# The tails of three weight loads are split by rows into pieces that use 3 to 15 DMA engines

## The chip, the cores and the metric

The kernel runs on one core of a Trainium2 chip, in one launch. The metric is the device time of that core in microseconds; lower is better. All data is 32-bit floating point. The time of before is the median of two runs.

## The reference

One decoding step of a block with two branches, for a batch of two sequences with one new token each and a width of 448. The first branch is attention with 16 query heads of size 256 over 8 cached key and value heads of 4,096 positions; the second is a bilinear gated unit with 1,792 hidden columns.

```python
xn = layernorm(x)
q = (xn @ wq), 16 heads of 256
p = softmax(q @ k_cache^T / 16)        # each key head serves two query heads
s = (p @ v_cache) @ wo
g = silu(((xn @ w_gate) * (xn @ w_up)) @ w_down)
out = x + s * g
```

Nearly all of the bytes are the two caches: 2 x 8 x 4,096 x 256 numbers each, 67 MB a cache. The weights are 24 MB.

## The kernel before

The work is 16 pairs of a key head and a sequence. For pair i the kernel needs `k{i}` (128 rows of 8,192 numbers) and `v{i}` (the same). They come in an order that lets one load serve two pairs: a load of 8 MB brings `v{i}` and `k{i+1}` as 128 rows of 64 KB. There are 14 of these (`vk` in the profile), into two buffers of the pool `ring`; the first key head (`first`) and the last pieces (`last0`, `last1`) are loaded by themselves.

The weights share one buffer, `slot`, one after the other: `wq0` (the queries of the first four key heads), `wg wu` (gate and up, 128 rows of 12,544 numbers, named `wgu`), `wd` (6,272 numbers a row), `wq1` and `wo` (10,752 numbers a row, three quarters of the output projection; the last quarter comes with `last1`). A weight lies in its rows as blocks of columns, and the matmuls go through the blocks in order.

`wq1` is a special case. A part of it, 256 KB, is taken out of the load of 128 rows and comes as `wqx` into 16 rows, from a source that is laid out as four times four rows with a gap, so that it isn't one run of rows.

All loads but that of `x` are issued by SyncE, in the order of the list `todo`, by the function `issue`. SyncE stops at an issue until the buffer is free: until the loads that wrote it have landed and the matmuls that read it are done. As `ring` has two buffers, one load is as a rule in flight when the next is issued behind it.

For each pair the loop does, in this order on TensorE: the values of pair i (`values`, line 274), the scores of pair i+1 (`scores`, line 243), then the softmax with VectorE and ScalarE, then whatever weight stage belongs to this i: `ffn_in` after pair 0 (line 171 with tile `s`), `ffn_out` after pair 2, `query(1)` after pair 4, `project` after pair 8. `project` for the blocks 16 to 23 of `wo` runs after the loop. The end of the kernel is the last value load in three pieces, the last quarter of the output projection (line 307), two VectorE operations and the store.

A load of `issue` is cut by columns only, at the places in `cuts`; each piece takes all 128 rows:

```python
for lo, hi in zip(cuts, cuts[1:]):
    nc.sync.dma_start(t[:, lo:hi], src[:, lo:hi])
```

Of the kernel before, what the change touches and what calls it, by code (L numbers as in the profile page):

```python
# [29 lines left out]
SIDE = 16  # L30
EXTRA = 8
EPS = 1e-5

# [4 lines left out]
def gated_decode_block(ctx: ExitStack, tc: tile.TileContext, x, first, vk, last0, last1, wq0, wq1, wqx, wo, wgu, wd, out):  # L40
    nc = tc.nc
# [20 lines left out]
    def issue(n=1):  # L62
        for names, src, cuts in todo[:n]:
            weight = names[0].startswith("w")
            if weight:
                t = slot.tile([128, PART], F32, name="slot", align_bytes=512)
            else:
                t = ring.tile([128, 2 * ROW], F32, name="ring", align_bytes=512)
            width = ROW if not weight else PART // len(names)
            for i, name in enumerate(names):  # L70
                loaded[name] = t[:, i * width:(i + 1) * width]
            for lo, hi in zip(cuts, cuts[1:]):
                nc.sync.dma_start(t[:, lo:hi], src[:, lo:hi])  # L73
            if names == ["wq1"]:
                at = src.shape[1]
                loaded["wqx"] = t[:, at:at + EXTRA * 512]
                nc.sync.dma_start(loaded["wqx"][:SIDE], wqx[:, :4])
        del todo[:n]
# [11 lines left out]
    plan(f"k{LAST + 1} v{LAST}", last0, [0, ROW, 2 * ROW])  # L90
    plan(f"v{LAST + 1} wo2", last1, [0, 4096, 7168, *(ROW + i * D for i in (0, 3, 5, 7, 8))])
    issue(3)


# [20 lines left out]
    nc.vector.scalar_tensor_tensor(sq, xc, 1.0, xc, op0=OP.mult, op1=OP.mult, accum_out=st[:, 2:3])  # L115
    nc.vector.tensor_scalar(st[:, 3:4], st[:, 2:3], 1.0 / D, EPS, op0=OP.mult, op1=OP.add)
    rstd = const.tile([B, 1], F32)
# [16 lines left out]
    for j in range(NK):  # L134
        at = 384 + j * SIDE
# [65 lines left out]
    def lift(ps):  # L201
        t = work.tile([128, D], F32, name="h")
        nc.scalar.copy(t, ps[:, :D])
        return t
# [108 lines left out]
    oT2 = const.tile([128, 1, 2, REP, W], F32)  # L313
    ss = scores(0)
    issue(2)
    p = over(softmax(*ss))
    for i in range(LAST):
        g, b = divmod(i, B)
        o = bank("o", 1)
        values(i, p[0], o)  # L320
        ss = scores(i + 1)

        issue(1 + (i + 1 in weights))
        nc.scalar.activation(ob[:, b * 4 + g if g < 4 else b * 3 + g - 4], o, AF.Copy, scale=p[1])  # L324
        if i == LAST - 1:
            cb = combine(ob, 6)
        p = softmax(*ss)
        if i < LAST - 1:
            p = over(p)
        if i == 7:  # L330
            cb = combine(ob, 8)
            for n in range(B):
                turn(oT0, cb[:, n * 256:(n + 1) * 256], 0, n, 4)
            ob = work.tile([128, 8, 512], F32, name="ob", bufs=1)
        if i in weights:
            if i == 0:
                ffn_in()
            if i == 2:
                ffn_out()
            if i == 4:  # L340
                query(1)
            if i == 8:
                project(oT0, 0, 0, EARLY)
# [6 lines left out]
    t = lift(wide)  # L350
# [72 lines left out]
```

## Time and profile before

| what | us |
|---|---|
| median of the runs | 376.75 (376.61 to 376.9) |
| the profiled execution | 376.31 |
| its span, first to last instruction | 374.5 |
| TensorE busy | 212.2 |
| VectorE busy | 63.2 |
| ScalarE busy | 36.2 |
| share of the span in which the 16 DMA engines are busy with SyncE's queue | 98.2% |

The profile is of one execution. Its busy times are sums over an engine's instructions; a DMA share is the mean over the sixteen DMA engines. A packet is one row of a transfer, or the small write that reports its completion. PE is TensorE's matmul, PEld its weight load, DVE VectorE, ACT ScalarE, SPq SyncE's sequencer, which issues the loads. Queue q1 holds SyncE's transfers, q10 the load of `x` that ScalarE issues, q8 and q14 the fetches of instructions.

### The profile page before, as it was taken

The page shows a single profiled execution, that of the slowest core. Times are in us where ns is not written, and L with a number is a line of the kernel's source. Part 1 is how long each engine was busy: PE and PEld are TensorE (multiplying, and loading weights), DVE is VectorE, ACT ScalarE, POOL GpSimd, SP SyncE. Part 2 cuts the span into 40 slices and gives each one's busy share as a digit, 9 for nine tenths or more (in the row PEclk, how much of TensorE's full clock was granted, in tenths as well). Part 3 has the DMA queues.
Part 4 walks back from the last instruction along what each step waited for, and adds up shares of the span by engine and source line. Part 5 has one row for each costly group of instructions (what it writes and reads, how often), then busy time and mean ns, then how long its engine had stood idle before and what let it go on. Part 6 is the DMA issues. An engine that isn't in the chain of part 4 may idle for free.

```text
span 374.5 us, 3254 instructions
## 1 busy us (share of the span) xinstructions
PE 212.2 (57%) x1464; PEld 62.4 (17%) x1464; DVE 63.2 (17%) x113; ACT 36.2 (10%) x56; POOL 1.2 (0%) x7
## 2 busy tenths in 40 slices
PE   1650648083762918699374666641718191909795
PEld 0110112021210202112021212200202020202232
DVE  4012030103030030300303030300211203020431
ACT  1001010001012020100101010100010101010120
POOL 1000000000000000000000000000000000000000
PEclk9986596657686786766857687765968776877899
DMA  8998999998999999999999999999999999999994
GB/s 343 441 469 378 444 453 448 448 443 377 428 443 448 434 400 447 436 441 450 420 448 441 443 394 423 444 448 441 448 400 443 448 427 413 450 409 437 409 417 184
DMA packets 4357, 158.79 MB, mean 424 GB/s; under 512 B 614, under 2 KB 744, under 8 KB 1256
## 3 DMA queue, kind: packets, MB, share of 16 engines
q1 hardware_dynamic: 4340, 158.59, 98.2%
q8 instruction: 11, 0.18, 0.2%
q14 instruction: 2, 0.02, 0.0%
q10 hardware_dynamic: 4, 0.00, 0.0%
HBM read 158.54 MB, written 0.06 MB: 423 GB/s over the span
## 4 chain that ended last, share of the span: by engine, by line
DMA 73%; PE 24%; SPq 1%; DVE 1%; issue 0%; ACT 0%; ACTq 0%
DMA ring<-vk 67%; PE o L274 12%; PE s L243 7%; DMA ring<-last 5%; PE t L177 2%; PE t L171 1%; SPq L73 1%; PE t L180 1%; DVE m L244 0%; ACT p L258 0%; PE acc L307 0%; DVE mx L251 0%; PE sm L266 0%; DVE h L371 0%; PE sm L249 0%
## 5 line engine op out<-in xcount | busy, mean ns | idle before, releaser
L274 PE MATMUL o<-ring,pT 128*32 128x512 f32 x480 | 83.4, 858 | 85.4 <-DMA ring<-vk 85.4
L243 PE MATMUL s<-ring,qT 128*32 128x512 f32 x512 | 61.1, 619 | 4.7 <-DMA ring<-first 3.1
L244 DVE TENSOR_REDUCE m<-s 128x1 f32<-128x1024 f32 x16 | 19.6, 1224 | 217.5 <-PE s L243 217.5
L274 PEld LDWEIGHTS o<-ring,pT 128*32 128x32 f32 x480 | 21.0, 150 | 139.7 <-issue 139.6
L324 ACT ACTIVATE ob<-o,su 128x512 f32<-128x512 f32 x14 | 9.6, 688 | 194.4 <-PE o L274 194.4
L258 ACT ACTIVATE p<-s,m 128x1024 f32<-128x1024 f32 x16 | 17.8, 1114 | 94.8 <-DVE m L255 94.8
L243 PEld LDWEIGHTS s<-ring,qT 128*32 128x32 f32 x512 | 17.7, 114 | 45.1 <-issue 43.5
L260 DVE STREAM_TRANSPOSE pT<-p 128x1024 f32<-128x1024 f32 x16 | 19.9, 1245 | 22.5 <-ACT p L258 22.5
L266 PE MATMUL sm<-su,add_head 128*128 128x1 f32 x32 | 7.3, 299 | 22.9 <-ACT p L258 22.9
L249 PE MATMUL sm<-ident,m 128*1 128x128 f32 x16 | 4.3, 270 | 18.9 <-DVE m L244 18.8
L171 PE MATMUL t<-slot,xnT 128*32 128x512 f32 x48 | 10.4, 1039 | 4.3 <-DMA slot<-wq 4.3
L251 DVE TENSOR_REDUCE mx<-sm 1x128 f32<-1x512 f32 x16 | 10.9, 679 | 6.3 <-PE sm L249 6.3
L254 PE MATMUL sm<-one,mx 1*128 1x1 f32 x16 | 3.5, 220 | 12.4 <-DVE mx L251 12.4
L266 PEld LDWEIGHTS sm<-su,add_head 128*128 128x128 f32 x32 | 6.0, 234 | 25.3 <-ACT p L258 24.1
L171 PE MATMUL s<-slot,xnT 128*32 128x448 f32 x48 | 7.2, 748 | 2.8 <-DMA slot<-wgu 2.8
L177 PE MATMUL t<-slot,oT 16*32 16x512 f32 x16 | 7.4, 942 | 0.0
L301 PE MATMUL wide<-slot,oT 128*32 128x448 f32 x48 | 7.1, 747 | 0.0
L249 PEld LDWEIGHTS sm<-ident,m 128*1 128x1 f32 x16 | 1.3, 79 | 33.0 <-DVE m L244 32.3
L283 PE MATMUL cb<-ob,add_blocks 128*32 128x64 f32 (+2 forms) x64 | 5.7, 481 | 0.8 <-ACT ob L363 0.8
L193 DVE STREAM_TRANSPOSE qT<-t 128x256 f32<-128x256 f32 x4 | 1.6, 428 | 25.2 <-PE t L177 14.2
L225 PE MATMUL t<-slot,hT 128*32 128x448 f32 x28 | 4.9, 812 | 0.0
L254 PEld LDWEIGHTS sm<-one,mx 1*128 1x128 f32 x16 | 2.2, 136 | 15.4 <-DVE mx L251 15.4
(70 smaller groups left out, 54.0 us busy)
## 6 DMA issues: line engine op xcount, KB each, us to landing
ring<-last SPq DMA_DIRECT2D x2, 4096.0 KB, 25.0
slot<-wgu SPq DMA_DIRECT2D x1, 6272.0 KB, 38.6
slot<-wo SPq DMA_DIRECT2D x1, 5376.0 KB
ring<-first SPq DMA_DIRECT2D x1, 4096.0 KB, 20.3
slot<-wq SPq DMA_DIRECT2D x1, 3584.0 KB, 11.1
slot<-wq SPq DMA_DIRECT2D x1, 3328.0 KB, 35.4
slot<-wd SPq DMA_DIRECT2D x1, 3136.0 KB, 36.9
ring<-last SPq DMA_DIRECT2D x1, 2048.0 KB
```

Of the source, the lines that this page charges most:

```text
L171: nc.tensor.matmul(ps[W * c:W * (c + 1), :n], xnT[:, k, :], block(NT * k + c), start=k == 0, stop=False)
L177: nc.tensor.matmul(ps[W * c:W * (c + 1), :n], xeT[:, j, :], extra[:SIDE, at:at + n], start=False, stop=j == NK - 1)
L243: nc.tensor.matmul(s[W * c:W * (c + 1), h, :], q[:, d], k[:, h, d, c, :], start=d == 0, stop=d == 1)
L244: nc.vector.tensor_reduce(m[:, 0:1], s, axis=AX.XY, op=OP.max)
L251: nc.vector.tensor_reduce(mx, sm[:1, None, :128].rearrange("p o (c j) -> p o j c", c=NT).to_broadcast([1, NT, W, NT]), axis=AX.X, op=OP.max)
L254: nc.tensor.transpose(sm[:, 128:129], mx.rearrange("p c j -> p (c j)"), one)
L258: nc.scalar.activation(p, s, AF.Exp, bias=m[:, 1:2], scale=1.0 / 16, accum_out=su[:, 0:1])
L260: nc.vector.transpose(pT.rearrange("p h n -> p (h n)"), p.rearrange("p h n -> p (h n)"))
L266: nc.tensor.matmul(sm[:, 130:131], add_head.rearrange("p a r j -> p (a r j)"), su[:, 0:1], start=True, stop=True)
L274: nc.tensor.matmul(o[W * t:W * (t + 1), :], pT[:, h, at:at + 2 * W:2], loaded[f"v{i}"][:, e * 512:(e + 1) * 512], start=e < NT, stop=e >= ...
L301: nc.tensor.matmul(wide[W * t:W * (t + 1), :D], heads(oT, i, first), loaded["wo"][:, i * D:(i + 1) * D], start=i < NT, stop=i >= LATE - NT)
L324: nc.scalar.activation(ob[:, b * 4 + g if g < 4 else b * 3 + g - 4], o, AF.Copy, scale=p[1])
```

## The change

The loads of `wgu`, `wd` and `wo` lose their last 512, 256 and 512 columns. These follow directly behind the main part as strips of 256 columns (1 KB a row), and each strip comes as two loads of some of the rows: the first 108 and the last 20 of the 128, and so on. All other loads stay as they are, `wq1` and `wqx` too. No computing instruction is added, removed or moved; SyncE's list of loads grows by ten.

```diff
+NARROW = 256
+ENDS = {"wu": [(108, 20), (117, 11)], "wd": [(119, 9)], "wo": [(125, 3), (98, 30)]}
...
-            for lo, hi in zip(cuts, cuts[1:]):
-                nc.sync.dma_start(t[:, lo:hi], src[:, lo:hi])
+            parts = [(lo, hi, (128,)) for lo, hi in zip(cuts, cuts[1:])]
+            if names[-1] in ENDS:
+                (lo, hi, _), = parts
+                mid = hi - NARROW * len(ENDS[names[-1]])
+                parts = [(lo, mid, (128,))] + [(mid + j * NARROW, mid + (j + 1) * NARROW, rows)
+                                               for j, rows in enumerate(ENDS[names[-1]])]
+            for lo, hi, rows in parts:
+                at = 0
+                for some in rows:
+                    nc.sync.dma_start(t[at:at + some, lo:hi], src[at:at + some, lo:hi])
+                    at += some
```

The order of SyncE's loads after the change, from `wgu` on:

```
wgu 128 x 12032, 108 x 256, 20 x 256, 117 x 256, 11 x 256
vk, vk
wd 128 x 6016, 119 x 256, 9 x 256
vk, vk, wq1, wqx, vk, vk, vk, vk
wo 128 x 10240, 125 x 256, 3 x 256, 98 x 256, 30 x 256
vk x 5, last (9 pieces)
```

## The prediction

> **What bounds the kernel now.** I read the page first (busy shares, DMA queues, the chain that ended last), then the windows, then the DMA issues and SyncE's own timeline.
>
> ```profile
> span 374.5 us, 3254 instructions
> PE 212.2 (57%) x1464; PEld 62.4 (17%) x1464; DVE 63.2 (17%) x113; ACT 36.2 (10%) x56; POOL 1.2 (0%) x7
> DMA packets 4357, 158.79 MB, mean 424 GB/s; under 512 B 614, under 2 KB 744, under 8 KB 1256
> q1 hardware_dynamic: 4340, 158.59, 98.2%
> q8 instruction: 11, 0.18, 0.2%
> DMA 73%; PE 24%; SPq 1%; DVE 1%; issue 0%; ACT 0%; ACTq 0%
> ```
>
> TensorE is busy 57% of the span; the sixteen DMA engines are busy 98.2% of it with one queue, SyncE's. The PE pieces of the chain are release steps: a buffer comes free, the next load is issued and then lies in the queue behind another. The windows say the same, and show the end (columns: length, busy time of PE, PEld, DVE, ACT and POOL, clock, DMA share, GB/s):
>
> ```profile
> 40.00:366.00 326.00, 193.99 (x1292) 56.43 (x1294) 54.41 (x85) 32.81 (x51) 0.00 (x0) 0.74 1.00 433
> 366.00:367.00 1.00, 1.00 (x14) 0.35 (x8) 0.00 (x0) 0.00 (x0) 0.00 (x0) 1.00 1.04 427
> 367.00:368.00 1.00, 0.79 (x7) 0.00 (x0) 0.00 (x0) 0.16 (x1) 0.00 (x0) 1.00 0.92 366
> 368.00:369.00 1.00, 0.42 (x24) 0.42 (x28) 0.00 (x0) 0.53 (x1) 0.00 (x0) 1.00 0.71 272
> 369.00:370.00 1.00, 1.00 (x42) 0.72 (x32) 0.25 (x1) 0.00 (x0) 0.00 (x0) 1.00 0.45 177
> 370.00:371.00 1.00, 0.62 (x24) 0.35 (x16) 0.00 (x0) 0.00 (x0) 0.00 (x0) 1.00 0.18 70
> ```
>
> From 40 to 366 us the share is 1.00 at 433 GB/s, or 27.1 bytes per ns and engine: no engine is ever without work, and none waits for another. So each engine's finish is the sum of what it carries, and the kernel ends with the most loaded one. The share falls over some 3.5 us at the end: the engines finish unevenly. The last landing that TensorE waits for is at 370.48:
>
> ```profile
> 171.28 5.26 PE o L274 x32
> 176.54 3.49 PE s L243 x32
> 180.03 0.02 issue
> 180.04 28.88 DMA ring<-vk
> ...
> 350.07 20.41 DMA ring<-last
> 370.48 0.04 issue
> 370.52 1.01 PE acc L307 x24
> ```
>
> Until there the average engine stands idle 0.08 + 0.29 + 0.55 + (0.48 - 0.18) = 1.2 us. That is all that a perfect levelling could bring: 0.3%.
>
> The trace also keeps each packet (one row of a transfer) with start and length. The views don't print them one by one; I strung them into sixteen chains, each packet starting where one ended, which works because a 65,536-byte row repeats every 2,415 ns. A row of S bytes takes S x 0.0368 + 4.4 ns (70 ns at 1,792 bytes, 607 at 16,384). How far each chain is behind the earliest one where the load of `k15` begins:
>
> ```
> engines                                            us behind the earliest
> 4 that carry wqx                                   2.70 2.78 3.15 3.26
> 2 that serve two of q8's code fetches              3.34 1.52 (2.94 from 350 us)
> 6 that serve one code fetch                        1.37 1.54 1.56 1.58 1.69 1.70
> 4 with neither                                     0.00 0.14 0.14 0.37
> ```
>
> `wqx` put 2.43 us on its four chains in one step, a code fetch some 1.4 us on one. The end is thus shared by the four of `wqx` and the two that are fetched on twice.
>
> **The change part by part.** The loads in question and what SyncE does around them (start, length, instruction; a merged row spans its members):
>
> ```profile
> slot<-wgu SPq DMA_DIRECT2D x1, 6272.0 KB, 38.6
> slot<-wd SPq DMA_DIRECT2D x1, 3136.0 KB, 36.9
> slot<-wo SPq DMA_DIRECT2D x1, 5376.0 KB
> slot<-wqx SPq DMA_DIRECT2D x1, 256.0 KB
> 18.54 0.33 SPq L73 DMA_DIRECT2D slot<-wgu  x1
> 26.69 23.66 SPq L73 DMA_DIRECT2D ring<-vk  x2
> 66.22 0.33 SPq L73 DMA_DIRECT2D slot<-wd  x1
> 86.62 18.52 SPq L73 DMA_DIRECT2D ring<-vk  x2
> 114.54 0.80 SPq L77 DMA_DIRECT2D slot<-wqx  x1
> 199.96 0.40 SPq L73 DMA_DIRECT2D slot<-wo  x1
> 217.73 91.36 SPq L73 DMA_DIRECT2D ring<-vk  x5
> ```
>
> *Bytes.* The three loads lose five tails of 128 rows x 1 KB; ten new loads carry the same 640 rows. No byte is added. Each of the 128-row loads runs on all engines, so a tail was 8 KB on each, 40 KB in all, or 1.51 us.
>
> *Engines.* How many a load uses shows in its completions. Of the 614 packets under 512 bytes, 128 are rows of the output and 2 belong to the load of `x`; the other 484 are completions, 30 x 16 for the thirty loads and stores of 128 rows and 4 for `wqx`, whose source is 4 x 4 rows: four engines, 64 KB each. So a load runs on the largest number up to 16 that divides its rows: 108 rows on 12 engines (9 rows each), 20 on 10 (2), 117 on 13 (9), 11 on 11 (1), 119 on 7 (17), 9 on 9 (1), 125 on 5 (25), 3 on 3 (1), 98 on 14 (7), 30 on 15 (2). If each takes the first so many in one fixed order, the 640 rows fall like this:
>
> ```
> place of the engine    1-3  4-5  6-7  8-9  10  11  12  13  14  15  16
> rows of 1 KB, after     74   73   48   31  30  28  27  18   9   2   0    (before: 40 KB each)
> ```
>
> A 1 KB row takes 37.7 + 4.4 = 42.1 ns, a completion some 7. Places 1 to 3: 74 x 42.1 + 10 x 7 = 3.19 us against 1.51, so +1.7 us; places 4 and 5: +1.6; 6 and 7: +0.6; 8 to 12: -0.15 to -0.35; 13 to 16: -0.7, -1.1, -1.4, -1.5.
>
> *Which engines.* No row says what places the four of `wqx` have, so the term is bounded from both sides: they are the first four (+1.6 to +1.7 on chains that share the end now), or the last four (-0.7 to -1.5, with the end left to others). I take the first: `wqx` is itself such a load of few engines, the nearest thing in the trace to the new ones, and the same hardware path picks for both. [...] The count of completions bears out the number of engines; which ones, no row here shows.
>
> *SyncE's queue.* `wqx`, on four engines, took 0.80 us to issue where a whole load took 0.33, so I price each new issue at 0.8: four behind `wgu` end at 22.1 us, the next load on the queue is issued from 26.69; two behind `wd` end at 68.2, the next is at 86.62; four behind `wo` end at 203.6, the next is at 217.73. Nothing queued behind them is late. Without that cover it would be 3.2 us at one place, still less than the load in flight.
>
> *New waits.* TensorE waits for the tails only ahead of the last blocks of `wu`, `wd` and `wo`: some ten waits on loads that lie in the queue directly behind the main part. PE's own reserve covers that (waited for: us in total, times, longest):
>
> ```profile
> PE o L274 <- DMA ring<-vk: 85.4, 13, 13.1
> PE s L171 <- DMA slot<-wgu: 2.8, 1, 2.8
> ```
>
> It stands 85 us before thirteen key and value loads. A tail of `wgu` that lands 1 us later still lies ahead of the last `wu` blocks, as the `wg` blocks come first.
>
> *Starving the fast engines.* The tightest issue is at 180.04: the earliest chain finishes its previous rows at 185.9, 5.9 us later. By then only `wgu` and `wd` have run, and the first seven places are 0.8 us later (39 rows of 1 KB where 24 KB were), so some 5 us are left. At the end the last pieces are issued 1.65 us later, against chains that finish the load before them from 353.3 us on, at least 2 us after the last issue. This costs nothing.
>
> *Sum.* The latest `wqx` chains end 1.65 us later, and what follows the last landing (some 4 us) stays: the profiled execution goes from 376.31 us (its span of 374.5 and 1.8 around it) to 377.96. The median of the runs is 0.44 above the profiled one, so 376.75 + 1.65 = 378.4 us, or +0.4%. That is inside the 2% that a measurement of this kernel can about tell from no change.
>
> **The rivals.**
>
> *Other engines.* The new loads start where the four idle-most chains are, and `wqx`'s four lie late in the order. Those four then gain 0.7 to 1.5 us; the chain with two fetches keeps its 3.3, less 0.15 to 0.35 if it is at places 8 to 12, plus 0.6 at 6 or 7. From -0.3 to +0.6: I put 376.5 us, with 375.5 as the floor from the 1.2 us above. For it: the two chains that start right after the two packets of `x` are not `wqx`'s. Against it: a start order blurred by up to 0.8 us.
>
> *Writes that meet.* In a whole load each engine writes rows of its own; the new pieces let an engine write rows that another engine writes at the same time in its large load. If a row's way into SBUF carries no more than one engine's 27.1 bytes per ns, every foreign row costs its 37.7 ns again: some 70 of the 74 rows, 2.6 us, so +4.3 us in all and 381.0 us; with the 40 rows that others push into the chain's own way, 1.5 more: 382.5. For it: 433 GB/s is flat whatever is in flight. Against it: nothing in this trace has two engines on one way. [...]
>
> *A stall per small load, the slower side.* Each of the ten pieces breaks the stream on its engines as the very first load does: its first rows take 1.2 to 2.2 us instead of 1.06, on average some 0.7 us lost. Ten such stalls on the first three chains: 7 + 1.65 = 8.7, so 385.4 us (+2.3%). It decides from (7.5 - 1.65) / 10 = 0.6 us per piece. Against it: the last seven loads, of 16 KB rows and less, follow each other 6 ns apart on a chain, and the window at 366 still has a share of 1.04.
>
> **How the numbers follow.** Forecast 0.60; other engines 0.22; writes that meet 0.12; stalls 0.06. The range goes from 376.3 to 381.0: it holds the forecast with its own spread (377.9 with no cost per row, 379.5 with two microseconds' worth of overlap at the ports), most of the second case, and reaches the third's price. Over 2% slower means above 384.3: the stalls and a little of the ports, 0.08. Over 2% faster means below 369.2; with 1.2 us to be had there is no way to it but an error of mine: 0.02. Within 2%: 0.90.
>
> **What would show it.** Right: the DMA share still 1.00 up to 366 us; over 100 more packets under 512 bytes (98 to 100 completions, as 12 + 10 + 13 + 11 + 7 + 9 + 5 + 3 + 14 + 15 = 99) and 640 more between 512 bytes and 2 KB; a longer slope at the end, with the share below 0.5 for about 3 us instead of 1.5; issues of about 0.8 us on SyncE. If the slope gets shorter and the span falls, the places were the other way round. If the share exceeds the bytes (1.00 at less than 433 GB/s) in the slices around 55, 100 and 240 us, rows meet on their way. If it drops below 1.00 there, pieces stall. A wait of TensorE on `slot` longer than now would say that the cover was misread.

## The result, and the profile after

The changed kernel takes 382.3 us (two runs, 380.53 and 384.08) against 376.75: a ratio of 1.015, with a 95% interval of 1.012 to 1.018. It is slower, by less than 2%, but by 5.55 us, over three times the 1.65 us of the forecast, and it lies above the range (376.3 to 381.0). The ratios here leave out any execution over 1.5% above the fastest of its kernel; in two of the experiments that drops slow stretches which belong to the kernel itself, so their single times are given too.

The profiled execution is the slower of the two, 384.08 us. From its page:

```profile
span 382.1 us, 3269 instructions
DMA packets 5096, 158.79 MB, mean 416 GB/s; under 512 B 713, under 2 KB 1483, under 8 KB 1995
q1 hardware_dynamic: 5079, 158.59, 97.8%
DMA 73%; PE 21%; another core or an unknown queue 3%; SPq 1%; issue 0%; DVE 0%
```

The bytes are the same and the engines are as busy as before, for 7.6 us longer: 416 GB/s instead of 424. The 99 new completions are there (614 to 713), so the pieces do run on as many engines as the largest divisor up to 16 says, and so are the 640 rows of 1 KB (130 to 770 packets between 512 bytes and 2 KB).

Two things are new in the windows (columns as above; the last two are the DMA share and GB/s, both counted by the packets that start in the window, so in a short one the second over the first is the rate of a working engine set). The stretches behind the three split loads:

```profile
54.00:58.00 4.00, 1.38 (x10) 0.76 (x14) 1.28 (x2) 0.00 (x0) 0.00 (x0) 0.58 1.13 393
58.00:83.00 25.00, 12.13 (x88) 2.96 (x84) 1.27 (x2) 0.53 (x1) 0.00 (x0) 0.66 1.02 396
104.00:109.00 5.00, 3.95 (x40) 0.97 (x32) 0.99 (x1) 0.69 (x1) 0.00 (x0) 1.00 1.13 434
240.00:249.00 9.00, 5.34 (x44) 1.91 (x40) 3.36 (x5) 1.76 (x3) 0.00 (x0) 0.82 1.07 387
110.00:240.00 130.00, 80.81 (x476) 22.27 (x480) 20.36 (x34) 14.16 (x22) 0.00 (x0) 0.72 1.00 431
249.00:370.00 121.00, 67.33 (x474) 20.31 (x466) 20.66 (x31) 11.24 (x19) 0.00 (x0) 0.73 1.00 430
```

The same two first windows of before:

```profile
54.00:58.00 4.00, 1.13 (x7) 0.55 (x11) 1.30 (x2) 0.06 (x1) 0.00 (x0) 0.65 1.20 520
58.00:83.00 25.00, 14.60 (x100) 3.65 (x96) 1.27 (x2) 0.53 (x1) 0.00 (x0) 0.65 0.97 420
```

The engines are not idle (share 1.02 to 1.13) but move 348, 388, 384 and 362 GB/s while they work (393 / 1.13 and so on), where before it was 433 in both. Elsewhere the rate is as ever. In the packet records rows of 64 KB take up to 3.5 us in these stretches instead of 2.42, on all sixteen chains alike. Summed over the execution, rows take 6.5 us per engine longer than the quickest of their size; before it was 1.5. That is 5.0 of the 7.6 us.

The end, and SyncE's timeline:

```profile
372.00:373.00 1.00, 0.63 (x24) 0.40 (x20) 0.25 (x1) 0.00 (x0) 0.00 (x0) 1.00 0.86 350
373.00:374.00 1.00, 1.00 (x10) 0.24 (x4) 0.00 (x0) 0.00 (x0) 0.00 (x0) 1.00 0.76 308
374.00:375.00 1.00, 1.00 (x8) 0.14 (x4) 0.00 (x0) 0.00 (x0) 0.00 (x0) 1.00 0.52 197
375.00:376.00 1.00, 0.21 (x6) 0.08 (x8) 0.00 (x0) 0.69 (x1) 0.00 (x0) 1.00 0.37 143
376.00:377.00 1.00, 1.00 (x48) 0.86 (x52) 0.25 (x1) 0.00 (x0) 0.00 (x0) 1.00 0.29 115
377.00:378.00 1.00, 0.58 (x22) 0.34 (x20) 0.00 (x0) 0.00 (x0) 0.00 (x0) 1.00 0.13 50
...
18.45 1.98 SPq L84 DMA_DIRECT2D slot<-wgu  x5
28.27 21.99 SPq L84 DMA_DIRECT2D ring<-vk  x2
203.90 1.91 SPq L84 DMA_DIRECT2D slot<-wo  x5
223.36 92.63 SPq L84 DMA_DIRECT2D ring<-vk  x5
```

The slope is longer. With the last landing on the chain at 377.82, the average engine is idle for 0.14 + 0.24 + 0.48 + 0.63 + 0.71 + (0.82 - 0.13) = 2.9 us before it, where it was 1.2: the unevenness grew by 1.7 us, as the forecast had it. SyncE needs 1.98 us for the five loads of `wgu` and is long done when the next is due.

So the term that was forecast is there, and a second one beside it. The experiments separate them.

### The profile page after: what moved, and what is told of

It is laid out like the page before. It is cut to its first block, busy times and chain, and to the rows that moved or that the text cites. A ratio compares the mean times of both kernels' runs of the same rounds, so it can differ in the third digit from the quotient of the medians.

```text
span 382.1 us, 3269 instructions
## 1 busy us (share of the span) xinstructions
PE 212.4 (56%) x1464; PEld 62.6 (16%) x1464; DVE 63.2 (17%) x113; ACT 36.2 (9%) x56; POOL 1.2 (0%) x7
## 4 chain that ended last, share of the span: by engine, by line
DMA 73%; PE 21%; another core or an unknown queue 3%; SPq 1%; issue 0%; DVE 0%
DMA ring<-vk 55%; PE o L286 11%; DMA slot<-wgu 10%; PE s L255 6%; DMA ring<-last 6%; DMA slot<-wq 3%; PE s L183 2%; PE t L183 1%; SPq L84 1%; PE s L196 0%; PE t L196 0%; PE acc L319 0%; DVE h L383 0%; DVE h L384 0%
## 5 line engine op out<-in xcount | busy, mean ns | idle before, releaser
L255 PE MATMUL s<-ring,qT 128*32 128x512 f32 x512 | 62.4, 630 | 5.1 <-DMA ring<-first 3.5
L183 PE MATMUL t<-slot,xnT 128*32 128x512 f32 x48 | 9.7, 971 | 4.1 <-DMA slot<-wq 4.1
L183 PE MATMUL s<-slot,xnT 128*32 128x448 f32 x48 | 7.1, 744 | 2.6 <-DMA slot<-wgu 2.6
```

The source lines that it names most:

```text
L183: nc.tensor.matmul(ps[W * c:W * (c + 1), :n], xnT[:, k, :], block(NT * k + c), start=k == 0, stop=False)
L255: nc.tensor.matmul(s[W * c:W * (c + 1), h, :], q[:, d], k[:, h, d, c, :], start=d == 0, stop=d == 1)
```

## Experiments

**The changed kernel again.** No edit.

> The changed kernel once more. Its two runs lie 3.5 us apart (380.53 and 384.08) where those of before lie 0.3 apart, and its profile has stretches (54 to 83, 104 to 110, 240 to 249 us) in which all sixteen DMA engines move rows slower at once. If these stretches belong to the change: every run above 380, the profile again with DMA at under 405 GB/s in the stretch behind wgu. If they were a chance of that one execution: most runs at 378.4 (the load of the last-ending engines alone, +1.65) and the profile at 430 GB/s or more in that stretch.

Measured: 380.49, 379.77, 380.30 and 385.34 us, median 380.39, ratio 1.013 (1.007 to 1.019). The profile is of the first:

```profile
54.00:58.00 4.00, 0.97 (x6) 0.53 (x10) 1.30 (x2) 0.14 (x2) 0.00 (x0) 0.65 1.23 454
58.00:83.00 25.00, 13.63 (x92) 3.40 (x88) 1.27 (x2) 0.53 (x1) 0.00 (x0) 0.65 1.01 438
237.00:246.00 9.00, 5.34 (x44) 1.93 (x40) 3.36 (x5) 1.89 (x3) 0.00 (x0) 0.83 1.07 402
```

A slow stretch stands behind `wgu` (369 GB/s while working) and `wo` (376), but here the first is over by 60 us, where in the recorded profile it went on to 83. Neither expectation fits alone: the short stretches belong to the change, and they cost 1.7 us (rows 3.2 us per engine over their quickest, 1.5 before). The long one is in one of the two profiles of this kernel: in the recorded one it adds 3.3 us of slow rows (6.5 against 3.2). The 385.34 has no profile, so that it had such a stretch too is not shown. A usual execution is 380.4.

**The strips without the split.**

```diff
-ENDS = {"wu": [(108, 20), (117, 11)], "wd": [(119, 9)], "wo": [(125, 3), (98, 30)]}
+ENDS = {"wu": [(128,), (128,)], "wd": [(128,)], "wo": [(128,), (128,)]}
```

> The same five strips of 256 columns, each as one load of all 128 rows (8 rows of 1 KB on every engine), so no piece uses fewer engines. If the 1 KB rows or the five more loads themselves cost: a good part of the +5.5 us, 379 to 382. If it is the pieces of some of the rows (uneven engines, or rows written in another engine's way): 5 x 8 x 4.4 ns + 5 x 7 ns = 0.2 us, so 377.0, and no slow stretch.

Measured: 376.88 against 376.45, ratio 1.001 (1.000 to 1.002).

```profile
54.00:58.00 4.00, 2.17 (x14) 1.07 (x18) 1.30 (x2) 0.59 (x2) 0.00 (x0) 0.50 1.39 586
237.00:246.00 9.00, 5.34 (x36) 1.82 (x32) 3.36 (x5) 1.21 (x2) 0.00 (x0) 0.69 1.08 457
```

586 / 1.39 = 422 and 457 / 1.08 = 423: no slow stretch. Rows of 1 KB and five more loads cost 0.4 us. The cause is in the pieces of some of the rows.

**Even pieces, other rows.**

```diff
+ENDS = {"wu": [(16, 112), (16, 112)], "wd": [(16, 112)], "wo": [(16, 112), (16, 112)]}
```

> [...] If rows meet on their way into SBUF: slow stretches behind wgu and wo, 379 or more. If uneven engines are the cause: 0.3 us, 377.0, and a flat 430 GB/s.

Measured: 378.93 (378.85 to 379.21), ratio 1.0065 (1.005 to 1.008).

```profile
54.00:58.00 4.00, 1.03 (x8) 0.46 (x12) 0.81 (x2) 0.00 (x0) 0.00 (x0) 0.51 1.32 508
237.00:246.00 9.00, 5.34 (x37) 1.71 (x32) 3.36 (x5) 1.21 (x2) 0.00 (x0) 0.77 1.08 401
```

385 and 371 GB/s while working: the slow stretches are back although 16 and 112 both divide by 16, and so, by the divisors that the 99 completions of the change bear out, every engine carries the same. Against the strips without a split it is 2.05 us. At the end the average engine now stands idle no longer than before (1.2 us in the last 12 us up to the last landing, by the packet records; 1.3 before, 2.8 in the repeated run of the change), so the longer slope came from the uneven pieces. For the slow stretches uneven engines are not needed. What is left against the strips is that the rows are dealt out to the engines differently (which row goes to which engine, no trace shows), and that there are ten loads in place of five; the runs below part the two.

**One engine alone.**

```diff
+ENDS = {"wd": [(127, 1)]}
```

> Only wd's strip, as 127 rows and 1 row: both run on one engine, which gets 128 rows of 1 KB, 128 x 42.1 ns = 5.4 us, where it had 0.3. It tells which engine comes first in the order. If wqx's four are the first ones: that chain also carries wqx, ends 5.1 us later than a wqx chain does now, about 381.5. If they are the last ones: it is a chain with neither wqx nor code fetches, 3 us ahead, and the end moves by 2 us, about 378.5. If small rows written in the way of other engines slow these: DMA under 420 GB/s between 100 and 110 us with rows of 64 KB that take longer than 2.42 us on many chains.

Measured: 381.35, 386.39, 387.66 and 403.12 us. The first two alone give a ratio of 1.020 (1.012 to 1.027). In the packet records the chain with the 128 rows of 1 KB is one of the four that later carry `wqx`, and its lead row of the next load starts 4.1 us behind the first. So one engine serves both loads, and it is one of `wqx`'s, as the forecast's choice of places has it. The trace has no engine numbers: that loads take their engines in one fixed order is the forecast's assumption, which this run fits and doesn't show.

The profiled 381.35 fits the 381.5 that this chain's rows give. But the edit does a second thing, which no expectation had. SyncE spends 34.1 us on the issue of the one-row load, up to 101.19 us, just after the 127 rows begin to move at 100.90. So the next load is issued at 101.29, where before it was 86.62. Thirteen of the other chains have run dry by then (from 100.62 to 100.94 us), their next rows start at 102.27 or later (share 0.18 in the first window), and rows then run slowly (454 / 1.30 = 349 GB/s while working in the second window). In this run a late issue is thus mixed with the rows of the one engine.

```profile
L84 SPq DMA_DIRECT2D slot<-wd x3: 328/339/34114, 66.3 to 67.1; - x3
...
66.30 34.89 SPq L84 DMA_DIRECT2D slot<-wd  x3
101.29 3.95 SPq L84 DMA_DIRECT2D ring<-vk  x2
...
100.00:102.00 2.00, 2.00 (x24) 0.59 (x20) 0.00 (x0) 0.54 (x1) 0.00 (x0) 1.00 0.18 74
102.00:106.00 4.00, 2.83 (x28) 0.67 (x20) 1.10 (x1) 0.15 (x1) 0.00 (x0) 1.00 1.30 454
```

The scatter up to 403 was not expected either.

**More load on the same engines, in the rows of `wqx`.** On the kernel before:

```diff
                 nc.sync.dma_start(loaded["wqx"][:SIDE], wqx[:, :4])
+                nc.sync.dma_start(t[:SIDE, at + EXTRA * 512:PART], wqx[:, :4, :PART - at - EXTRA * 512])
```

> The kernel before, with 1,792 of wqx's 4,096 columns loaded a second time, to an unused place of the same 16 rows. Four engines get 4 more rows of 7 KB each, 4 x 268 ns = 1.07 us, and write only rows that are their own in a whole load (wqx left no slow stretch). It is the load of the last-ending engines alone, without rows that meet. If uneven engines cost what they carry: 376.45 + 1.07 = 377.5, or 0.1 to 0.5 less where another chain ended last, and 430 GB/s throughout. If getting out of step is by itself what slows all engines: 379 or more, with a slow stretch behind wqx (150 to 175 us).

Measured: 377.74 against 376.46, +1.28, ratio 1.003 (1.002 to 1.005). In this run the uneven engines cost what they carry (1.07 and 0.2 more) and slow nobody: 440 / 1.02 = 431 GB/s.

```profile
149.00:156.00 7.00, 3.34 (x28) 1.15 (x20) 2.47 (x4) 1.21 (x2) 0.00 (x0) 0.85 1.02 440
```

**The same load to other rows.** From the run above:

```diff
-                nc.sync.dma_start(t[:SIDE, at + EXTRA * 512:PART], wqx[:, :4, :PART - at - EXTRA * 512])
+                nc.sync.dma_start(t[128 - SIDE:, at + EXTRA * 512:PART], wqx[:, :4, :PART - at - EXTRA * 512])
```

> As the run with wqx's 1,792 columns loaded a second time (377.74), the same four engines, rows and bytes, but to rows 112 to 127 of the buffer, also unused there, instead of rows 0 to 15. Only whose way the bytes take differs. If rows that meet are what slows: the four engines move their 28 KB at half speed and hold up the owners, 1.07 us more at the end, 378.8, and a dip of the DMA rate below 420 GB/s behind wqx, at 149 to 153 us. If only the load of the engines counts: 377.7 again and 433 GB/s.

Measured: 379.71 (379.45 to 379.83) against 376.36, ratio 1.009 (1.007 to 1.010): 2.0 us above the run with rows 0 to 15. Same source, same number of engines, same bytes, same rows in number: the destination alone differs.

```profile
149.00:156.00 7.00, 3.34 (x32) 1.11 (x25) 3.16 (x4) 1.20 (x2) 0.00 (x0) 0.98 1.05 382
```

382 / 1.05 = 364 GB/s where it was 431. This shows that it matters where an engine writes, apart from how much and from where it reads, and is the cleanest of the pairs. Not only the four engines pay: in the packet records their 7 KB rows take up to 0.59 us instead of 0.27, and the lead rows of the next load on the other twelve take 3.2 to 4.2 us instead of 2.42. The price, 2.0 us, is about twice the 1.07 us that the expectation had for four engines at half speed, and it falls on all sixteen engines, here as in the other runs. The rows are not slow in themselves, as whole loads write them too at 433 GB/s (before, 40 to 366 us). Which rows an engine writes in a whole load stands in no trace, so that rows 0 to 15 are the own rows of `wqx`'s engines and these rows belong to others is the reading that fits the runs, not one that a row shows.

**Four times the bytes to other rows.** The even pieces with `NARROW = 1024`.

> The mixed strips of 16 and 112 rows, 1,024 columns wide instead of 256: four times the bytes that land in another engine's way, in the same number of rows and loads. If each row or byte that meets another costs its share: 4 x 2.5 = 10 us, about 386. If each load costs a fixed jam: 2.5 us again, 379. If the slow stretches keep themselves up once begun: times that scatter by several us, and stretches under 400 GB/s that last long after the pieces have landed.

Measured: 386.29 (385.41 to 386.49) against 376.46, +9.8, where 10 was expected from bytes; ratio 1.026 (1.024 to 1.027).

```profile
52.00:60.00 8.00, 4.64 (x24) 1.84 (x28) 2.14 (x4) 1.20 (x2) 0.00 (x0) 0.58 1.20 382
239.00:250.00 11.00, 7.34 (x56) 2.46 (x52) 3.36 (x5) 1.75 (x3) 0.00 (x0) 0.75 1.07 277
```

318 and 259 GB/s while working. The cost goes with the bytes, not with the number of rows or loads: 160 KB per engine would take 6.0 us at 27.1 bytes per ns, and taking 0.4 off for the strips (measured with rows of 1 KB) they cost 9.4 more; with 40 KB it was 1.5 and 2.05. In these two runs each such byte cost every engine 1.4 to 1.6 times its own transfer time again.

**To catch a long stretch.** `ENDS = {"wu": [(127, 1)]}`.

> The one-engine pieces of 127 rows and 1 row behind wgu instead of behind wd, where the times scattered from 381 to 403 us. It is to catch a long slow stretch in a profile. If the slow stretch keeps itself up with whole rows alone: rates of 330 to 400 GB/s that go on for 10 us and more after the last 1 KB row, and times that scatter again. If it lasts only while the small rows are in flight: 381.5, back at 433 GB/s within some 2 us of the last small row.

Measured: 399.33 and 381.41 us; the profile is of the first. SyncE is held up here too, 36.65 us over the three loads of `wgu`: the next load is issued at 55.41, where before it was 26.69, after most engines have run dry (from 54.3 us on, by the packet records), and its rows start at 56.4. The share of 0.56 below is no idleness: it leaves out the rows that start just before 57 us.

```profile
18.67 36.65 SPq L84 DMA_DIRECT2D slot<-wgu  x3
55.41 0.83 SPq L84 DMA_DIRECT2D ring<-vk  x2
...
57.00:62.00 5.00, 5.00 (x28) 1.10 (x24) 0.00 (x0) 0.00 (x0) 0.00 (x0) 0.50 0.56 226
62.00:67.00 5.00, 3.88 (x40) 0.83 (x32) 0.46 (x1) 0.53 (x1) 0.00 (x0) 0.99 0.97 419
70.00:150.00 80.00, 34.50 (x240) 10.51 (x240) 10.35 (x16) 9.04 (x13) 0.00 (x0) 0.73 1.00 387
150.00:235.00 85.00, 50.35 (x268) 13.29 (x272) 10.85 (x17) 5.68 (x9) 0.00 (x0) 0.66 1.00 387
238.00:300.00 62.00, 30.11 (x216) 9.09 (x208) 10.86 (x17) 5.12 (x9) 0.00 (x0) 0.79 1.01 437
```

The small rows are done by 60 us, the rate is back at 419 / 0.97 = 432, and at 68 us it falls to 387 GB/s and stays there, to three digits, for some 167 us in which nearly all rows are those of loads of 128 rows. Then it is 433 again. Rows take 18.7 us per engine longer than the quickest of their size in this execution, where before it was 1.5; that is about the 17.9 us between the two times. So in this execution a slow stretch went on long after the small rows had landed; no execution of before or of the strips without the split showed one. In the packet records it ends at 236.8 us, where a code fetch on one engine ends (235.7 to 236.8); in the recorded profile of the changed kernel the rate is 387 as well and it ends at 83.0, during a fetch (82.7 to 83.7). Five other fetches in between did not end it, so that a fetch ends it is not shown. What begins it, what keeps it up and why at eight ninths of the rate stays open.

**Levelling without the change's pieces.** An attempt at a version that beats both: `wqx` with 32 rows over 8 engines.

```diff
-SIDE = 16
+SIDE = 32
+SPLIT = 2
...
```

The rest of the edit (left out) gives `wq1` 12 blocks of 512 columns instead of 13 and `wqx` 8 x 4 rows of 4,096 numbers instead of 4 x 4, with the matmuls to match.

> The same aim as the change, to level the engines, but only with rows written in an engine's own way: wqx has 32 rows of 16 KB instead of 16, from a source of 8 x 4 rows, so 8 engines take 64 KB each; wq1 loses 1,024 columns instead of 512. Every engine saves 8 x 2 KB more than before (0.60 us), the first eight carry 2.43 us; TensorE does 8 matmuls of 32 rows instead of 12. If engines end by what they carry and the code fetches lie on the other eight: the chains with two fetches end 0.6 us earlier, the first eight 0.6 earlier than wqx's four do now: 375.85. If the fetches fall on the first eight too: up to 1.8 us later, 378. If rows of this kind do meet: a slow stretch behind wqx and 378 or more.

Measured: 376.65 (376.44 to 378.13) against 376.46, ratio 1.002 (1.001 to 1.003): no gain. No slow stretch either, but the eleven times fall into two groups, seven at 376.4 to 376.8 and four at 378.0 to 378.1. In the packet records two of the eight engines that serve code fetches are among the eight of `wqx`; one ends 4.1 us behind the earliest. That is the expectation's second case, fetches on the first eight too. What makes the two groups of times is not shown. No version faster than the kernel before was found.

## Why the prediction was wrong

*What bounds the kernel, bytes, cover of the issues, waits:* right. No new wait on `slot` shows (`PE s L183 <- DMA slot<-wgu` 2.6 us, 2.8 before), and the ten issues are hidden; a piece of the change costs SyncE 0.3 to 0.45 us, half of the 0.8 that was taken from `wqx`. That price is no rule: behind a piece of 127 rows on one engine an issue took 34.1 us.

*Engines and their places:* right as far as the runs go. The count of completions fits (99 more), the single-engine run put both its loads on one of `wqx`'s engines, which fits an order that starts there and doesn't show it, and the end became uneven by 1.7 us where 1.65 was forecast; with even pieces it did not. The rival "other engines" is out. The uneven part alone was tested at 1.07 us and measured 1.28.

*The step that failed* is the sum's silence on rows that meet. The sum took 0 for it, since no row of the trace had two engines on one way, and left it to a rival with a chance of 0.12. The even pieces measure 2.05 us for the same 640 rows, and the changed kernel's usual execution shows 1.7. The range and its chances also count on an overlap at ports; no run shows a port, and what the runs showed in its place is these 2.05 us, and 2.0 us between two runs that differ in the destination alone. The strips without the split cost 0.4 us, of which the forecast's price per row and completion gives 0.2 and is in its sum already. So 1.65 for the uneven end, 0.2 more for the strips and 1.7 to 2.05 for the slow rows give 3.6 to 3.9 us, and the usual execution is 3.9 above before: 380.4, the price of that rival (381.0) but for 0.6. The rival's own working was right in that the destination has a price and wrong in where it falls: it charged the first chains 2.6 us, and 1.5 more for rows that others push into their way; the runs show all sixteen slowed at once. That the 381.0 lies so near the usual 380.4 is therefore partly luck.

*The stalls per small load:* out for the pieces of the change. The share in the stretch is 1.13, so rows are slow and engines are not idle. The idle engines of the single-engine run are no such stall: their next load was issued late.

*What no step had:* the long stretch at 387 GB/s. It makes up 3.3 of the 3.7 us between the usual 380.4 and the recorded 384.08, and so lifts the median of the two first runs to 382.3.

The range failed on this stretch: it stopped at the rival's central price and left no room for a cost that lasts longer than its cause. Two usual executions would have fallen inside it, but with slow rows in them and not by the uneven end alone.

## What to carry to other kernels

The rows of a load did more in these runs than to set how many DMA engines carried it (99 completions for the ten pieces); where the load landed mattered too: the same bytes on the same number of engines cost 1.28 us in rows 0 to 15 and 3.35 us in rows 112 to 127. The author's reading, which no row shows, is that such a load sends engines into rows that others write in the large loads. Measured in the even pieces, with 433 GB/s around them, is that each byte of these strips cost all engines 1.4 to 1.6 times its own transfer time again. Where engines are to be levelled, put the data where it slowed nobody here (rows 0 to 15 as `wqx` has them) and count the background fetches first (eleven in the profile of before, some 1.4 us each on its chain). After such a change read SyncE's own timeline: behind 127 rows on one engine an issue was held up for 34.1 us. A cost that the trace has no row for is not zero: run the smallest kernel that has it before the sum is closed.

## What the runs showed of the hardware that was not expected

In two profiles the sixteen engines, each with a full queue, fell into a steady 387 GB/s instead of 434 (64 KB rows in 2.71 us instead of 2.42 in the profile of the changed kernel) and stayed there with nearly nothing but loads of 128 rows in flight: for 27 us in the changed kernel and for some 167 in the run with 127 rows and 1 row behind `wgu`. Single times of one kernel lay up to 21.8 us apart (381.35 to 403.12, the same pieces behind `wd`); that such a stretch made the longest of them is not shown, as it has no profile. Behind a load of 127 rows on one engine, SyncE stood 34.1 us at the issue of the next small load in one run and 35.9 us in another, until just after the 127 rows began to move. The load after it was issued at 101.29 us instead of 86.62, and at 55.41 instead of 26.69; thirteen of the engines in the first run and most of them in the second had run dry by then.
